# RWKV-6 attention and mixture of depths on one core: order of the state update, the gate's arithmetic, and where groups of product pieces end

## The chip, the cores and the metric

The kernel runs on one core of one Trainium2 chip, in FP32 but for a few BF16 comparison tables. The core has a matrix engine (TensorE; "PE" in the profile, with "PEld" for its weight loads), a vector engine (VectorE, "DVE"), a scalar engine (ScalarE, "ACT"), a general one (GpSimd, "POOL") and a queue for transfers (SyncE, "SP"). Each works through its own list of instructions in order, and they meet at semaphores. The metric is the device time of one execution in microseconds; each quoted time is a median over executions.

## The reference

Batch is 4, with 8 heads, 768 steps and 48 channels per head. The first part is a recurrence with a decaying state for each head, the second lets the 128 best of the 768 rows of each batch through a two-layer network.

```python
for t in range(S):                                   # attention
    cur = einsum('bhd,bhe->bhde', u[None] * kt, vt)
    y[:, :, t] = einsum('bhd,bhde->bhe', rt, state + cur)
    state = wt[:, :, :, None] * state + einsum('bhd,bhe->bhde', kt, vt)

x = y as rows of H*D = 384 values                    # bridge
scores = einsum('bsd,d->bs', x, w_gate)
for b in range(B):                                   # mixture of depths
    top_idx = argpartition(-scores[b], 128)[:128]
    xe = x[b, top_idx]                               # 128 x 384
    ye = maximum(xe @ w1, 0.0) @ w2                  # 384 -> 1024 -> 384
    g = 1.0 / (1.0 + exp(-scores[b, top_idx]))
    out[b, top_idx] = xe + g[:, None] * ye           # other rows: out = x
```

## The kernel before, in words

**Chunks and turns.** The 768 steps of a batch are cut into 6 chunks of 128 steps, so there are 24 chunks. The program is one long sequence of calls of `turn(i)`, i from -2 to 24, whose order is written by hand; every engine gets its instructions in that order. Turn i works on several chunks at different stages. In the order of the calls: `own_products(i+1)` (POOL), `scores(i)` (PE: products of R and K into the PSUM tile `ps_s`), `masked(i)` (DVE: two multiplications by a triangular mask, L292), `carry(i-1)` (DVE: `mid`, L379, the sum of the chunk's product tile `ps_kv` and the old state; then POOL multiplies by the decay, L380; for the first chunk of a batch DVE does it in one multiplication, L382; for the last there is nothing), `scaled(i+1, "K")` (PE transposes, DVE multiplies, L258), `back(i)` (PE transposes K back, ACT copies it out as `kt`, L297), `rows_out(i-1)` (PE `ps_y`, ACT, POOL, and the store), `row_products`, `compared_t(i-2)` (PE transposes the row scores into `ps_e`, L400), `own_values(i)` (ACT L270, POOL `vo` L274), `compared(i-2)` (DVE counts the larger scores), then one step of `mixture` and a first portion of network pieces, `scaled(i+1, "R")`, `decays_t(i+2)`, `outputs_t(i)` (PE L310 and L318, ACT `yt` L323), `carry_products(i)` (PE `ps_kv`), a second portion of pieces, `scans(i+2)` (DVE: two scans over the decays, L227 and L239, with two small operations between), `range_check(i+2)`, `row_sums(i-1)` (ACT L345) and a second step of `mixture`.

**PSUM.** The tiles `ps_kv` and `ps_e` share one bank (pool `psK`, one buffer), so `ps_e` of a turn can be written once `carry` has read `ps_kv`. The four kinds of transposes use two banks of `psT`. The network's `ps_h` and `ps_f` share one bank, `psM`, except in the last batch.

**The mixture.** `mixture(b)` is a generator, started when the last chunk of batch b is compared, and resumed twice per turn. Its steps are: rank, pick, the indices and the gathering of the 128 rows `xe` (an indirect transfer issued by POOL), an empty step, the transposes `xeT`, and the gate. The gate step computes the row score of `xe` again and the sigmoid of it, with exp of minus its absolute value: a multiply-and-sum over 384 columns (L482), four operations on one column each (L487, L492, L493, L495), one more (L498) on DVE and one exp on ACT (L490). Then the batch goes to the list `picked`. Counted from the turn in which the last chunk was compared, the gate falls into the third turn after it: turns 10, 16 and 22. For the last batch all this follows behind the turns.

**The pieces.** `forward(b)` is the network as a generator of 16 pieces. Eight are "h" pieces (three matrix products each); after every fourth, ACT empties the bank into `hid` with Relu (L516). Eight are "f" pieces (one product of 384 columns each, accumulated in the bank); after the last, DVE forms `ye` (L527) and POOL scatters it (L530). `fed(n)` takes n pieces from the batch in hand, or from the next one in `picked`. `fed_in_turn` calls it with 1 in the first portion of a turn and with 2 in the second (`PIECES` is 3); for the last batch but one it only takes one per turn.

**The end.** After turn 24 the last chunk is compared, four pieces run, the last batch is ranked, four more pieces run ahead of its indices, the rest of the third batch while its rows are fetched, and then the whole network of the last batch, alone.

Of the kernel before, what the change touches and what calls it, by code (L numbers as in the profile page):

```python
# [10 lines left out]
FP32 = mybir.dt.float32  # L11
# [3 lines left out]
AF = mybir.ActivationFunctionType  # L15
ALU = mybir.AluOpType
AX = mybir.AxisListType

L = 128
# [19 lines left out]
def kernel(  # L39
# [39 lines left out]
    nc = tc.nc  # L79
# [3 lines left out]
    C = H * D  # L83
# [14 lines left out]
    lev = ctx.enter_context(tc.tile_pool(name="lev", bufs=2))  # L98
    mod = ctx.enter_context(tc.tile_pool(name="mod", bufs=1))
# [43 lines left out]
    wg_bc = consts.tile([L, C], FP32)  # L143
# [276 lines left out]
    def mixture(b):  # L420

        every, ahead, lost = against.pop(b)
        ps = psT.tile([L, NCH], FP32, tag="t", name="ps_r")
        for c in range(NCH):
            for e in range(c, NCH):
                nc.tensor.matmul(
                    ps[:, c:c + 1], ahead[:, e, c * L:(c + 1) * L], ones[:, 0:1],
                    start=(e == c), stop=(e == NCH - 1),
                )
        rank = mod.tile([L, NCH], FP32, name="rank", bufs=2)  # L430
        nc.vector.tensor_add(rank, lost[:, :, 0], lost[:, :, 1])
        nc.vector.tensor_add(rank, rank, behind_n)
        nc.vector.tensor_sub(rank, rank, ps)
        yield

        for gi, (c0, n) in enumerate(groups):

            pick = mod.tile([L, NCH, L], BF16, name="pick")
            at = rank
            if c0 > 0:  # L440
                at = mod.tile([L, NCH], FP32, name="at")
                nc.vector.tensor_scalar_add(out=at, in0=rank, scalar1=float(-c0))
            nc.vector.tensor_tensor(
                out=pick, in0=_heads(slots, NCH), in1=at.to_broadcast([L, NCH, L]),
                op=ALU.is_equal,
            )
            yield
            ps = psT.tile([L, 2], FP32, tag="t", name="ps_i")
            for c in range(NCH):
                nc.tensor.matmul(  # L450
                    ps, pick[:, c, :], ids[:, b, c, :], start=(c == 0), stop=(c == NCH - 1)
                )
            while len(picked) + len(feed) > 1:
                fed(1)
            idx = mod.tile([L, 1], UINT32, name="idx", bufs=2)
            nc.vector.tensor_scalar(
                out=idx, in0=ps[:, 0:1], scalar1=ps[:, 1:2], scalar2=float(b * S),
                op0=ALU.add, op1=ALU.max,
            )
            rows = views[b][0:b + 1].rearrange("b s c -> (b s) c")  # L460
            where = bass.IndirectOffsetOnAxis(ap=idx[0:n, 0:1], axis=0)
            xe = mod.tile([L, C], FP32, name="xe", bufs=2)
            if n < L:
                nc.vector.memset(xe, 0.0)
            nc.gpsimd.indirect_dma_start(
                out=xe[0:n], out_offset=None, in_=rows, in_offset=where,
                bounds_check=(b + 1) * S - 1, oob_is_err=False,
            )
            yield
            yield  # L470

            ps = psT.tile([L, NDC, L], FP32, tag="t", name="ps_x")
            for dc in range(NDC):
                nc.tensor.transpose(ps[:, dc, :], xe[:, dc * L:(dc + 1) * L], ident)
            xeT = mod.tile([L, NDC, L], FP32, name="xeT", bufs=2)
            nc.scalar.copy(out=xeT, in_=ps)
            yield


            own = mod.tile([L, 1], FP32, name="own", bufs=2)  # L480
            scr = lev.tile([L, C], FP32, tag="scr", name="scr")
            nc.vector.tensor_tensor_reduce(  # L482
                out=scr, in0=xe, in1=wg_bc, scale=1.0, scalar=0.0, op0=ALU.mult, op1=ALU.add,
                accum_out=own,
            )
            neg = mod.tile([L, 1], FP32, name="neg", bufs=2)
            nc.vector.scalar_tensor_tensor(  # L487
                out=neg, in0=own, scalar=-1.0, in1=own, op0=ALU.mult, op1=ALU.min
            )
            nc.scalar.activation(out=neg, in_=neg, func=AF.Exp)  # L490
            den = mod.tile([L, 1], FP32, name="den", bufs=2)
            nc.vector.tensor_scalar_add(out=den, in0=neg, scalar1=1.0)  # L492
            nc.vector.reciprocal(out=den, in_=den)  # L493
            gate = mod.tile([L, 1], FP32, name="gate", bufs=2)
            nc.vector.scalar_tensor_tensor(  # L495
                out=gate, in0=own, scalar=0.0, in1=neg, op0=ALU.is_ge, op1=ALU.max
            )
            nc.vector.tensor_mul(gate, gate, den)  # L498
            picked.append((b, n, rows, where, xe, xeT, gate))
            yield  # L500

    def forward(b, n, rows, where, xe, xeT, gate):

        hid = mod.tile([L, NFC, L], FP32, name="hid")
        for f0 in range(0, NFC, 4):

            pool, tag = (psY, "y") if b == B - 1 and f0 % 8 == 4 else (psM, "m")
            ps = pool.tile([L, 4, L], FP32, tag=tag, name="ps_h")
            for q in range(4):
                for dc in range(NDC):  # L510
                    nc.tensor.matmul(  # L511
                        ps[:, q, :], w1[:, dc, (f0 + q) * L:(f0 + q + 1) * L],
                        xeT[:, dc, :], start=(dc == 0), stop=(dc == NDC - 1),
                    )
                if q == 3:
                    nc.scalar.activation(out=hid[:, f0:f0 + 4, :], in_=ps, func=AF.Relu)  # L516
                yield

        ps = psM.tile([L, C], FP32, tag="m", name="ps_f")
        for fc in range(NFC):  # L520
            nc.tensor.matmul(  # L521
                ps, hid[:, fc, :], w2[:, fc, :], start=(fc == 0), stop=(fc == NFC - 1)
            )
            if fc < NFC - 1:
                yield
        ye = mod.tile([L, C], FP32, name="ye", bufs=2)
        nc.vector.scalar_tensor_tensor(  # L527
            out=ye, in0=ps, scalar=gate, in1=xe, op0=ALU.mult, op1=ALU.add
        )
        nc.gpsimd.indirect_dma_start(  # L530
            out=rows, out_offset=where, in_=ye[0:n], in_offset=None,
            bounds_check=(b + 1) * S - 1, oob_is_err=False,
        )
        yield


    work = {}
    mixing, picked, feed = [], [], []

    def step(f, n, *more):  # L540
        if 0 <= n < N:
            f(work.setdefault(n, dict(n=n)), *more)
# [7 lines left out]
            except StopIteration:  # L550
                mixing.pop(0)

    def fed(n):

        while n > 0:
            if not feed:
                if not picked:
                    return
                feed.append((picked[0][0], forward(*picked.pop(0))))
            try:  # L560
                next(feed[0][1])
                n -= 1
            except StopIteration:
                feed.pop(0)

    def fed_in_turn(n):

        if (feed or picked) and (feed or picked)[0][0] == B - 2:
            n = min(n, 1) if n < PIECES - PIECES // 2 else 0
        fed(n)  # L570

    PIECES = -(-2 * NFC * len(groups) // NCH)


    def turn(i):
        step(own_products, i + 1)
        step(scores, i)
        step(masked, i)
        step(carry, i - 1, work.get(i))
        step(scaled, i + 1, "K", k_bufs, "right")  # L580
        step(back, i)
        step(rows_out, i - 1, i == N)
        if i == N:
            row_scores_soon(work[N - 1], work[N - 1]["x"])
        else:
            step(row_products, i - 1)
        step(compared_t, i - 2)
        step(own_values, i)
        step(compared, i - 2)
        mix()  # L590
        fed_in_turn(PIECES // 2)
        step(scaled, i + 1, "R", r_bufs, "left")
        step(decays_t, i + 2)
        step(outputs_t, i)
        step(carry_products, i)
        fed_in_turn(PIECES - PIECES // 2)
        step(scans, i + 2)
        step(range_check, i + 2)
        if i < N:
            step(row_sums, i - 1)  # L600
        if 0 <= i - 2 < N and chunks[i - 2][1] == NCH - 1:
            mixing.append(mixture(chunks[i - 2][0]))
        mix()
        if i > -2:
            loads(i + 5)
        if i > 1:
            load_weights(1 if NCH > 2 else 100)
# [17 lines left out]
    def general(gen):  # L625
        u_t = gen.tile([D, H], FP32, name="u_t")
        nc.sync.dma_start(out=u_t, in_=u.rearrange("h d -> d h"))
        for b in range(B):
# [34 lines left out]
            for _ in mixture(b):  # L663
                pass
# [8 lines left out]
        out=wide, in0=ps[0:1, 0:1], scalar1=0.0, scalar2=None, op0=ALU.is_gt  # L673
# [30 lines left out]
```

## Time and profile before

| what | value |
|---|---|
| time, median of 3 runs | 237.0 us (235.15 to 237.57) |
| span of the profiled execution | 235.7 us |
| PE busy, share of the span | 87% |
| DVE busy | 74% |
| ACT busy | 60% |
| POOL busy | 56% |
| chain that ended last, by engine | PE 55%, DVE 20%, ACT 9%, issue 8% |

The starts of the turns can be read from PE's first product of `scores` in each turn (the L283 rows of the timeline), in us from the span's start:

| turn | 2 | 5 | 7 | 9 | 10 | 11 | 12 | 13 | 14 | 15 | 16 | 17 | 18 | 22 | 23 |
|---|---|---|---|---|---|---|---|---|---|---|---|---|---|---|---|
| starts at | 25.46 | 45.45 | 57.18 | 72.08 | 80.19 | 89.01 | 98.32 | 106.46 | 115.74 | 124.65 | 132.41 | 141.24 | 150.56 | 184.65 | 192.29 |

So a turn takes 6 to 9.3 us. Turns 10 to 15 and 16 to 21 are the two batches in which attention and network pieces are mixed throughout (52.22 and 52.24 us), and from 199 us on only the end is left: it takes 36 us and is mostly one dependent chain.

In a row of the timeline the first number is the start in us, the second the time in us from the first to the last of the instructions merged in it, and the bracket is the engine's idle time just before, with what ended it. In a row of the waits the three numbers are the idle time in total, the number of waits, and the longest.

### The profile page before, as it was taken

What the parts mean: (1) busy time and instruction counts of PE and PEld (TensorE: products, weight loads), DVE (VectorE), ACT (ScalarE), POOL (GpSimd) and SP (SyncE); (2) the same over time, 40 slices, a digit from 0 to 9 for tenths busy, and PEclk for the clock granted to TensorE, in tenths of its full rate; (3) what the DMA queues carried; (4) which work ended last, traced back from release to release, by engine and by line L of the source; (5) the groups of instructions that cost most, each with busy time, mean ns of one, the idle gap of its engine ahead of it and who ended that gap; (6) DMA issues with size and microseconds to landing.
All of it is one profiled execution on the core that took longest, in us unless ns stands there. A gap on an engine that the chain in (4) does not pass through costs nothing.

```text
span 235.7 us, 6339 instructions
## 1 busy us (share of the span) xinstructions
PE 205.4 (87%) x2290; PEld 170.0 (72%) x2290; DVE 173.3 (74%) x386; ACT 141.0 (60%) x666; POOL 132.4 (56%) x153
## 2 busy tenths in 40 slices
PE   2889999999898997989999997989999987688960
PEld 2678888888687796877877886877777876665830
DVE  6977888999999799697697899788698873423010
ACT  6357788889787766677476657685576656111200
POOL 2364778877856983674467883584368845003010
PEclk9999999999999999999999999999999999799995
DMA  8999999998999785848946965956621101001001
GB/s 123 182 166 174 196 189 247 207 230 170 231 218 215 201 176 75 152 88 118 151 97 107 176 128 66 171 114 93 100 70 33 70 33 36 33 0 61 9 0 49
DMA packets 105655, 29.20 MB, mean 124 GB/s; under 512 B 100496, under 2 KB 104848, under 8 KB 105616
## 3 DMA queue, kind: packets, MB, share of 16 engines
q1 hardware_dynamic: 105104, 27.14, 65.2%
q0 software_dynamic: 512, 1.57, 2.2%
q8 instruction: 20, 0.33, 0.6%
q14 instruction: 19, 0.16, 0.2%
HBM read 23.20 MB, written 5.51 MB: 122 GB/s over the span
## 4 chain that ended last, share of the span: by engine, by line
PE 55%; DVE 20%; ACT 9%; issue 8%; DMA 3%; POOL 2%; POOLq 0%
PE ps_t L214 11%; PE ps_s L283 8%; PE ps_yt L310 7%; PE ps_f L521 7%; PE ps_yt L318 6%; PE ps_h L511 6%; PE ps_w L214 4%; DVE sc L292 4%; DVE left L239 3%; ACT kt L297 3%; PE ps_kv L364 3%; DVE right_buf L227 3%; DVE R L258 2%; PE ps_e L400 2%; ACT junk L249 2%
## 5 line engine op out<-in xcount | busy, mean ns | idle before, releaser
L270 ACT ACTIVATE rk<-rk 128x48 f32<-128x48 f32 x192 | 43.7, 236 | 0.0
L292 DVE TENSOR_TENSOR sc<-ps_s,before_f 128x512 f32<-128x512 f32 x48 | 30.8, 683 | 17.2 <-PE ps_s L283 17.2
L270 ACT ACTIVATION_READ_ACCUMULATOR rk<-rk 128x1 f32 x192 | 37.3, 194 | 0.0
L335 POOL TENSOR_TENSOR x<-x,vo 128x384 f32<-128x384 f32 x23 | 23.0, 1000 | 19.5 <-ACT x L334 19.5
L239 DVE TENSOR_TENSOR_SCAN left<-ps_w,from_left 128x511 f32<-128x511 f32 x24 | 30.7, 1281 | 0.9
L283 PE MATMUL ps_s<-R,K 48*128 48x128 f32 x384 | 29.0, 292 | 0.8 <-DVE R L258 0.7
L227 DVE TENSOR_TENSOR_SCAN right_buf<-ps_w,from_right 128x511 f32<-128x511 f32 x24 | 29.1, 1211 | 0.7 <-PE ps_w L214 0.6
L323 ACT COPY yt<-ps_yt 128x512 f32<-128x512 f32 x24 | 14.1, 586 | 24.1 <-PE ps_yt L318 21.4
L263 POOL TENSOR_TENSOR rk<-r_buf,k_buf 128x384 f32<-128x384 f32 x24 | 24.2, 1006 | 7.4 <-DMA r_buf<-in_r_dram 7.2
L511 PE MATMUL ps_h<-xeT,w 128*128 128x128 f32 x192 | 27.1, 292 | 1.3 <-ACT hid L516 0.7
L283 PEld LDWEIGHTS ps_s<-R,K 48*128 48x128 f32 x384 | 24.3, 194 | 4.0 <-issue 1.6
L310 PE MATMUL ps_yt<-sc,v_buf 128*64 128x128 f32 x384 | 27.1, 285 | 0.0
L340 POOL TENSOR_TENSOR scr<-x,wg_bc 128x384 f32<-128x384 f32 x23 | 25.5, 1108 | 1.8
L511 PEld LDWEIGHTS ps_h<-xeT,w 128*128 128x128 f32 x192 | 24.7, 204 | 2.3 <-ACT hid L516 0.9
L297 ACT COPY kt<-ps_t 128x512 f32<-128x512 f32 x24 | 14.0, 583 | 20.1 <-PE ps_t L214 20.0
L521 PE MATMUL ps_f<-w,hid 128*128 128x384 f32 x64 | 23.9, 499 | 2.1 <-ACT hid L516 2.1
L264 POOL TENSOR_TENSOR rk<-rk,u_bc 128x384 f32<-128x384 f32 x24 | 24.1, 1002 | 2.5 <-DMA u_bc<-in_u_dram 0.7
L310 PEld LDWEIGHTS ps_yt<-sc,v_buf 128*64 128x64 f32 x384 | 21.2, 140 | 4.1 <-issue 3.7
L380 POOL TENSOR_TENSOR state<-mid,all 128x192 f32<-128x192 f32 x16 | 8.1, 506 | 27.8 <-DVE mid L379 27.8
L318 PE MATMUL ps_yt<-R,state 64*48 64x128 f32 x320 | 21.5, 274 | 0.3 <-POOL state L380 0.3
L274 POOL TENSOR_TENSOR vo<-v_buf,own 128x384 f32<-128x384 f32 x24 | 19.9, 828 | 1.9 <-ACT rk L270 1.9
L214 PE MATMUL ps_w<-ident,w_buf 128*128 128x128 f32 x96 | 15.8, 291 | 4.8 <-DMA w_buf<-in_w_dram 4.2
(98 smaller groups left out, 390.2 us busy)
## 6 DMA issues: line engine op xcount, KB each, us to landing
w_buf<-in_w_dram SPq DMA_DIRECT2D x24, 192.0 KB, 4.6
k_buf<-in_k_dram SPq DMA_DIRECT2D x24, 192.0 KB, 4.7
r_buf<-in_r_dram SPq DMA_DIRECT2D x24, 192.0 KB, 4.9
v_buf<-in_v_dram SPq DMA_DIRECT2D x24, 192.0 KB, 4.2
out_dram<-x SPq DMA_DIRECT2D x24, 192.0 KB, 2.3
w<-in_moe_w_dram SPq DMA_DIRECT2D x3, 512.0 KB, 5.8
w<-in_moe_w_dram SPq DMA_DIRECT2D x4, 384.0 KB, 4.9
u_bc<-in_u_dram SPq DMA_DIRECT2D x1, 192.0 KB, 4.6
```

The costliest lines, as they stand in the source:

```text
L214: nc.tensor.transpose(ps[:, j, :], src(j), ident)
L227: nc.vector.tensor_tensor_scan(out=flat[:, W - 2::-1], data0=wt[:, W - 1:0:-1], data1=from_right.rearrange("p j t -> p (j t)")[:, W - 2::- ...
L239: nc.vector.tensor_tensor_scan(out=left.rearrange("p j t -> p (j t)")[:, 1:W], data0=wt[:, 0:W - 1], data1=start.rearrange("p j t -> p (j ...
L263: nc.gpsimd.tensor_mul(rk, r_bufs[n % NBUF][:, :, 0:D], k_bufs[n % NBUF][:, :, 0:D])
L270: nc.scalar.activation(out=rk[:, h, :], in_=rk[:, h, :], func=AF.Copy, accum_out=o[:, h:h + 1])
L283: nc.tensor.matmul(ps[:, par, j, :], t["K"][rows, j, :], t["R"][rows, j, :], start=True, stop=True,)
L292: nc.vector.tensor_mul(t["sc"][:, par], ps[:, par], _heads(before_f, HP))
L310: nc.tensor.matmul(ps[DP * par:DP * par + DP, j, :], vt[:, 2 * j + par, :], t["sc"][:, par, j, :], start=(j == 0), stop=(old is None), ski ...
L318: nc.tensor.matmul(ps[DP * par:DP * par + D, j, :], old[rows, j, :], t["R"][rows, j, :], start=False, stop=True, skip_group_check=True,)
L340: nc.gpsimd.tensor_mul(t["scr"], t.pop("x"), wg_bc)
L511: nc.tensor.matmul(ps[:, q, :], w1[:, dc, (f0 + q) * L:(f0 + q + 1) * L], xeT[:, dc, :], start=(dc == 0), stop=(dc == NDC - 1),)
L521: nc.tensor.matmul(ps, hid[:, fc, :], w2[:, fc, :], start=(fc == 0), stop=(fc == NFC - 1))
```

## The change

It has three parts, all of them in the order or the engine of work; what is computed stays the same.

1. `carry(i-1)` is called ahead of `scores(i)` and `masked(i)` instead of behind them, so on DVE `mid` stands in front of the two masks. It is meant to free the bank for `ps_e` and to start the state's update sooner.
2. The gate's score is formed by a product on POOL and a sum by ACT's accumulator, the exp is taken of the negated score directly, and two operations on one column are left on DVE (an addition with a cap at 3e38, and the reciprocal). A `yield` between the exp and these two puts them at the turn's end, behind the scans, and `picked` gets the batch half a turn later than before.
3. In the turns, a portion of pieces ends early at a piece whose bank is then emptied: the fourth h piece of a group, and the last f piece. It is meant to keep PE from waiting in front of the next piece for that emptying.

```diff
@@ mixture
+            scr = lev.tile([L, C], FP32, tag="scr", name="scr")
+            nc.gpsimd.tensor_mul(scr, xe, wg_bc)
             own = mod.tile([L, 1], FP32, name="own", bufs=2)
-            scr = lev.tile([L, C], FP32, tag="scr", name="scr")
-            nc.vector.tensor_tensor_reduce(
-                out=scr, in0=xe, in1=wg_bc, scale=1.0, scalar=0.0, op0=ALU.mult, op1=ALU.add,
-                accum_out=own,
-            )
-            neg = mod.tile([L, 1], FP32, name="neg", bufs=2)
-            nc.vector.scalar_tensor_tensor(
-                out=neg, in0=own, scalar=-1.0, in1=own, op0=ALU.mult, op1=ALU.min
-            )
-            nc.scalar.activation(out=neg, in_=neg, func=AF.Exp)
-            den = mod.tile([L, 1], FP32, name="den", bufs=2)
-            nc.vector.tensor_scalar_add(out=den, in0=neg, scalar1=1.0)
-            nc.vector.reciprocal(out=den, in_=den)
+            nc.scalar.activation(out=scr, in_=scr, func=AF.Copy, accum_out=own)
+            nc.scalar.activation(out=own, in_=own, func=AF.Exp, scale=-1.0)
+            yield
             gate = mod.tile([L, 1], FP32, name="gate", bufs=2)
-            nc.vector.scalar_tensor_tensor(
-                out=gate, in0=own, scalar=0.0, in1=neg, op0=ALU.is_ge, op1=ALU.max
-            )
-            nc.vector.tensor_mul(gate, gate, den)
+            nc.vector.tensor_scalar(
+                out=gate, in0=own, scalar1=1.0, scalar2=3e38, op0=ALU.add, op1=ALU.min
+            )
+            nc.vector.reciprocal(out=gate, in_=gate)
             picked.append((b, n, rows, where, xe, xeT, gate))
@@ forward
-                yield
+                yield q == 3
...
             if fc < NFC - 1:
-                yield
+                yield False
...
-        yield
+        yield True
@@ fed
-    def fed(n):
+    def fed(n, on=True):
...
-                next(feed[0][1])
+                last = next(feed[0][1])
                 n -= 1
+                if last and not on:
+                    return
@@ fed_in_turn
-        fed(n)
+        fed(n, on=False)
@@ turn
         step(own_products, i + 1)
+        step(carry, i - 1, work.get(i))
         step(scores, i)
         step(masked, i)
-        step(carry, i - 1, work.get(i))
         step(scaled, i + 1, "K", k_bufs, "right")
```

The instruction lists show what follows from part 2 for the pieces. A batch's pieces start one turn later: turns 10 and 16 lose the three h pieces that they had of the newly picked batch. Turn 13 now holds two h pieces (the second ends its portion) where it held three f pieces, turn 15 holds three f pieces instead of one, and turn 16 the last two f pieces of the batch before, with `ye` on DVE between the product R and the scans (before, `ye` stood in turn 15, ahead of R). Turns 17 to 22 repeat this. In turn 22 the last two f pieces replace one h piece, and the rest of the third batch is one piece later at the end, so that six f pieces instead of five stand between the last batch's indices and its transposes.

More of the change, by code (lines that the diff above doesn't have):

```diff
@@ L477, in mixture @@
             yield
+            scr = lev.tile([L, C], FP32, tag="scr", name="scr")
+            nc.gpsimd.tensor_mul(scr, xe, wg_bc)
             own = mod.tile([L, 1], FP32, name="own", bufs=2)
-            scr = lev.tile([L, C], FP32, tag="scr", name="scr")
-            nc.vector.tensor_tensor_reduce(
-                out=scr, in0=xe, in1=wg_bc, scale=1.0, scalar=0.0, op0=ALU.mult, op1=ALU.add,
-                accum_out=own,
-            )
-            neg = mod.tile([L, 1], FP32, name="neg", bufs=2)
-            nc.vector.scalar_tensor_tensor(
-                out=neg, in0=own, scalar=-1.0, in1=own, op0=ALU.mult, op1=ALU.min
-            )
-            nc.scalar.activation(out=neg, in_=neg, func=AF.Exp)
-            den = mod.tile([L, 1], FP32, name="den", bufs=2)
-            nc.vector.tensor_scalar_add(out=den, in0=neg, scalar1=1.0)
-            nc.vector.reciprocal(out=den, in_=den)
-            gate = mod.tile([L, 1], FP32, name="gate", bufs=2)
-            nc.vector.scalar_tensor_tensor(
-                out=gate, in0=own, scalar=0.0, in1=neg, op0=ALU.is_ge, op1=ALU.max
-            )
-            nc.vector.tensor_mul(gate, gate, den)
+            nc.scalar.activation(out=scr, in_=scr, func=AF.Copy, accum_out=own)
+            nc.scalar.activation(out=own, in_=own, func=AF.Exp, scale=-1.0)
+            yield
+            gate = mod.tile([L, 1], FP32, name="gate", bufs=2)
+            nc.vector.tensor_scalar(
+                out=gate, in0=own, scalar1=1.0, scalar2=3e38, op0=ALU.add, op1=ALU.min
+            )
+            nc.vector.reciprocal(out=gate, in_=gate)
             picked.append((b, n, rows, where, xe, xeT, gate))
```

## The prediction

> **What bounds the kernel now.** I read the page first, then PE's timeline for the length of each turn, then the waits, then all engines around turn 16, where a gate is computed.
>
> ```profile
> PE 205.4 (87%) x2290; PEld 170.0 (72%) x2290; DVE 173.3 (74%) x386; ACT 141.0 (60%) x666; POOL 132.4 (56%) x153
> ...
> PE   2889999999898997989999997989999987688960
> ```
>
> PE is busy nearly throughout until slice 33, so a turn can only shrink by the gaps that PE still has. The waits say which these are:
>
> ```profile
> DVE sc L292 <- PE ps_s L283: 17.2, 16, 1.9
> PE ps_e L400 <- DVE mid L379: 3.9, 4, 1.4
> PE ps_e L400 <- ACT kt L297: 3.1, 11, 0.3
> PE ps_f L521 <- ACT hid L516: 2.1, 3, 0.7
> PE ps_e L400 <- DVE state L382: 1.0, 1, 1.0
> ```
>
> `ps_e` needs nothing from `kt`; it needs the bank that `mid` reads, and `mid` ends within 0.05 us of `kt` in those 11 turns (28.23 against 28.27 us in turn 2). So the first row of `ps_e` and the second are one wait, for `mid`. DVE meanwhile waits 17.2 us in front of the masks: it has room there.
>
> The largest gaps come from the gate. Turn 16, DVE:
>
> ```profile
> 136.53 1.01 DVE L482 CUSTOM_DVE_ANT_0 scr<-xe,wg_bc 128x384 f32<-128x384 f32 x1
> ...
> 137.59 0.84 DVE L487 SCALAR_TENSOR_TENSOR neg<-own 128x1 f32<-128x1 f32 x1
> ...
> 139.25 0.93 DVE L498 TENSOR_TENSOR gate<-gate,den 128x1 f32<-128x1 f32 x1
> 140.10 0.68 DVE L258 TENSOR_TENSOR R<-ps_t,left 128x512 f32<-128x512 f32 x1
> ```
>
> From 136.53 to 140.10, 3.57 us, R and the two scans behind it stand still. The masks and `mid` of turn 17 are late for it, and PE has this gap in turn 17:
>
> ```profile
> 143.26 0.60 PE L214 MATMUL ps_y<-ident,yt 128*128 128x128 f32 x4
> 145.22 0.29 PE L400 MATMUL ps_e<-ident,score 128*128 128x128 f32 x1 [1.36 <-DVE mid L379]
> ```
>
> Why an operation on one column takes 0.9 us is seen on POOL:
>
> ```profile
> 138.37 0.82 POOL L274 TENSOR_TENSOR vo<-v_buf,own 128x384 f32<-128x384 f32 x1
> 139.16 1.00 POOL L263 TENSOR_TENSOR rk<-r_buf,k_buf 128x384 f32<-128x384 f32 x1
> ```
>
> L498 ends at 140.18, `rk` at 140.16. And ACT, whose next work after `yt` waits for the scans:
>
> ```profile
> 139.22 0.59 ACT L323 COPY yt<-ps_yt 128x512 f32<-128x512 f32 x1 [0.56 <-PE ps_yt L318]
> 142.35 0.19 ACT L238 COPY left<-from_left 128x1 f32<-128x1 f32 x1 [2.55 <-DVE from_left L235]
> ```
>
> **What the Trainium skill says.** "SBUF — State Buffer", section "Who interferes with whom": a DVE instruction with two SBUF inputs contends with a GpSimd instruction that reads SBUF, the later one is blocked to the other's end, and with at most one SBUF input it is free. The trace agrees: L498 (two inputs) takes 0.93 us beside `rk` and 0.16 us at the end, where POOL is idle; L492 and L493 (one input) take 0.15 and 0.16 us at every place. The two new DVE operations have one input each. "Trace Analysis", section "Per-engine timelines": the window of a DVE or ACT instruction leaves out its wait for semaphores, so a blocked instruction shows as idle time in front of it; the 2.55 us above are such a case. "ScalarE: Activation LUTs", section "Table sets: the hidden batching unit": cheap functions are in every set, so exp and copy share one; the trace agrees with one table load in all (1.28 us, at the start).
>
> **Part 1, `mid` in front of the masks.** It adds and removes nothing on DVE; `mid` (0.35 us, 0.26 us from start to start) moves into the idle time there. Gain on PE:
> - Turns 2 to 4: after `ps_e`, PE's next transposes need `kt`'s bank anyway. In turn 1, which has no `ps_e`, they start 0.05 us after `kt`; in turn 2 at 28.50, 0.23 us after it. Gain 0.17 us a turn, 0.5 us in all.
> - Turns 5 to 8 hang on DVE (the chain goes from masks to K, R, scans and masks again, from 46.66 to 66.40). A reordered queue that never idles gains nothing, but `mid` falls into the last idle time ahead of it: 0.3 us. The 1.03 us that PE saves in turn 7 (`state`, L382) are lost again in turn 9, where K's transposes wait for `idx` at the end of DVE's queue and the state on POOL stands behind the gathering. Up to turn 10: 0.8 us.
> - Turns 13 to 15 and 19 to 21: a piece follows `ps_e`, so the whole gap goes. From `ps_y` to `ps_e` it is 0.88 us in turn 14 (117.77 to 118.65) and 0.44 us in turn 12, where nothing waits. Gain 0.44 us each.
> - Turns 11, 17 and 23: see part 2.
>
> **Part 3, ends of portions.** In turn 12 PE waits from 104.77 (an h piece takes 0.77 us there) to 105.62 for `hid`: 0.85 us, and again in turn 18. Now an h piece stands in that place, and the bank's emptying is behind us: ACT finishes its own-values at 103.4, so `hid` ends at 104.0, where the next h piece starts. Gain 0.85 us each. The other such waits are in the end and stay.
>
> **Part 2, the gate.** Take turn 10 with its first score product as 0 (80.19 in the trace). DVE no longer does the gate and PE no longer the three h pieces (3 x 0.7 = 2.1 us, which return elsewhere). PE: `kt`'s transposes at 2.0 (they wait for `xeT`), `ps_e` 2.9, R's transposes 3.3, `yt` products 4.3 and 5.3, `ps_kv` 6.35, so turn 11 starts at 6.95 instead of 8.82. Then the new chain: POOL adds x at 3.7 (ACT's copy ends at 3.63), row product 4.8, `vo` 5.75, the new product 6.55 to 7.6 (1.0 us by the L340 row; 1.6 us at worst). ACT sums it (L345: 0.5 us) and takes exp (L490: 0.20 us): to 8.4. Behind these on ACT stand `yt`, `left`, the two range checks, the row sums and `kt` of turn 11: 2.5 us from `yt` to `kt` by turn 2 (24.98 to 27.5), so `kt` runs from 11.0 to 11.6, though PE wants it at 9.1. On DVE gate and reciprocal (0.2 us each with the wait between) hold `mid` until 9.1 and the masks until 9.35; `ps_e` 9.65, one h piece, then PE waits for `kt` until 11.65. Then 0.9 us of transposes, two times 1.02 of `yt` products, 1.5 of pieces: turn 12 starts at 16.15 instead of 18.13.
>
> Turn 16 has in addition two f pieces (0.65 and 0.7 us): turn 17 starts at 8.0. `ye` waits on DVE for the last of them, 8.05 to 8.7, and behind it the two scans, so `left` ends at 11.5, gate and reciprocal at 11.85, `mid` 12.2, masks 13.4. ACT's `left` waits for the reciprocal of the decays at 10.2, `kt` ends at 12.95. PE: `ps_e` 12.3, h piece, transposes 13.05, `yt` products 14.0; turn 18 starts at 17.6 instead of 18.15.
>
> The other turns: 12 takes 8.14 - 0.85 = 7.3; 13 has two pieces instead of three: 9.28 - 0.44 - 0.7 = 8.14; 14: 8.91 - 0.44 = 8.47; 15 has two pieces more: 7.76 - 0.44 + 1.39 = 8.71. Together 32.6.
> - Turns 10 to 15: 16.15 + 32.6 = 48.8, before 52.22: 3.4 us.
> - Turns 16 to 21: 17.6 + 32.6 = 50.2, before 52.24: 2.0 us.
> - Turns 22 to 24: by the same working `ps_y` of the last chunk comes at 13.4 from turn 22's start instead of 14.23: 0.8 us.
> - The end: six f pieces instead of five ahead of `ps_x`; the five end at 215.0, the rows arrive at 215.3, a piece takes 0.69: 0.4 us lost. The last gate lies beside the h pieces (5.6 us).
>
> Sum: 0.8 + 3.4 + 2.0 + 0.8 - 0.4 = 6.6 us; 237.0 - 6.6 = 230.4 us.
>
> **The rivals.**
> - The new waits take most of it: ACT's queue behind the sum and DVE's behind `ye` cost more than I worked out. For it: both stand in front of work that PE needs within 3 us, and POOL has been as late as 1.6 us for L340. If three gate turns lose 1.3 us more each, 234.3 us; that is where the batches gain little but the bank waits. 20%.
> - The new waits hide: if POOL runs the product sooner or PE reaches turn 11 later, `kt` is not late, which is worth up to (11.65 - 10.4) = 1.25 us in turn 11 and as much again in 17: 227.9 us. Against it: POOL's order is fixed, and `vo` waits for all eight own-values. 13%.
> - Nothing moves: PE is the bound and pieces are only pushed along. Against it: the gaps of 1.36, 0.85 and 0.44 us are idle time on PE. 237 us. 6%.
> - Slower: the pushed pieces meet the blocked scans, turns 16 and 17 grow beyond 18.15 by 2 us, and the end by one piece: 2 x 2 + 0.7 - 0.8 above the old time, 241 us. For it: `ye` stands ahead of both scans. 6%.
> - The forecast has the rest, 55%.
>
> **Range and chances.** From the hidden waits' 227.9 to the first rival's 234.3: 227.8 to 234.4 us leaves out the two last cases and the tails. Faster by over 1% means under 234.6 us: 55 + 13 + half of the 20, and a little of the spread, 0.79; within 1% 0.14; slower 0.07.
>
> **What would show it.** Right: no wait of `ps_e` for `mid` in turns 13 to 15; L487 and L490 at 0.15 us each; PE waits for `kt` of 1 to 2 us in turns 11 and 17; `ye` in turn 16 with idle time in front of it; turn 11 about 7 us after turn 10. Wrong: turn 18 later than 18.2 us after turn 16, or a `yt` so late that `ps_y` stops PE for over 1 us.

## The result, and the profile after

| | before | after |
|---|---|---|
| median of the first comparison (4 and 4 runs) | 236.07 us | 226.84 us |
| ratio, 95% interval | | 0.9624 [0.9536, 0.9712] |
| median of a later comparison (43 and 6 runs) | 235.39 us | 226.97 us |
| ratio, 95% interval | | 0.9599 [0.9548, 0.9649] |
| span of the profiled execution | 235.7 us | 225.0 us |

The ratios were estimated from the fast executions of each comparison and are not quotients of the medians, which take all of them (226.97 to 235.39 would be 0.964).

The kernel became 8.4 us faster by the medians of the larger comparison. The forecast was 230.4 us with a range down to 227.8, so the gain was larger than the forecast and the time fell below the range.

The page of the kernel after, busy times and PE's slices:

```profile
PE 201.2 (89%) x2290; PEld 167.7 (75%) x2290; DVE 165.2 (73%) x366; ACT 141.7 (63%) x674; POOL 135.6 (60%) x157
...
PE   2889999999999897999999996999999998688950
```

DVE lost 8 us of work and 20 instructions, POOL gained 3 us and ACT 0.7 us, and PE has fewer slices below 9 in the middle. The waits of the kernel after (engine and line, whom it waits for, us in total, times, longest):

```profile
DVE ye L522 <- PE ps_f L516: 17.2, 4, 7.5
...
ACT scr L483 <- POOL scr L481: 8.1, 4, 2.2
...
PE ps_e L400 <- ACT scr L345: 3.1, 2, 1.8
```

The rows of `ps_e` waiting for `mid`, `kt` and `state` are gone, as is PE's wait for `hid` inside the turns. In their place `ps_e` waits twice, 3.1 us in all, for the row sum of L345 on ACT. PE in turn 17 of the kernel after (start, duration; the bracket is the idle time ahead):

```profile
136.70 0.60 PE L214 MATMUL ps_y<-ident,yt 128*128 128x128 f32 x4
139.08 0.32 PE L400 MATMUL ps_e<-ident,score 128*128 128x128 f32 x1 [1.78 <-ACT scr L345]
```

These two rows answer to those of before with the wait of 1.36 us for `mid`. DVE and ACT show what led to it:

```profile
134.79 0.62 DVE L522 SCALAR_TENSOR_TENSOR ye<-ps_f,gate,xe 128x384 f32<-128x384 f32 x1 [3.22 <-PE ps_f L516]
135.32 1.21 DVE L227 TENSOR_TENSOR_SCAN right_buf<-ps_w,from_right 128x511 f32<-128x511 f32 x1
...
136.76 0.18 DVE L235 RECIPROCAL from_left<-all 128x4 f32<-128x4 f32 x1
...
138.18 0.13 DVE L487 TENSOR_SCALAR gate<-own 128x1 f32<-128x1 f32 x1
138.34 0.16 DVE L490 RECIPROCAL gate<-gate 128x1 f32<-128x1 f32 x1
```

```profile
134.14 0.52 ACT L483 ACTIVATE scr<-scr 128x384 f32<-128x384 f32 x1 [1.97 <-POOL scr L481]
...
136.98 0.19 ACT L238 COPY left<-from_left 128x1 f32<-128x1 f32 x1 [1.52 <-DVE from_left L235]
...
138.43 0.51 ACT L345 ACTIVATE scr<-scr 128x384 f32<-128x384 f32 x1
```

`ye` (L522) waits 3.22 us on DVE for PE's last f piece; e7 below tests whether the scans behind it could have run in that time. So L235 ends at 136.94, ACT's `left` starts at 136.98, and behind `left` and the two range checks stands the row sum (138.43), from which `ps_e` takes its operand. In turn 11 there is no `ye`, and the same wait (1.29 us) remains from ACT's sum of the gate alone, which waits 1.97 us for POOL.

Here is where the time went. The kernel before was run once more (`e4_before_again`), and its profile is used, since its matrix clock matches that of the kernel after; the sections are differences between the same rows of the two profiles:

| section | before (e4) | after | gained | forecast |
|---|---|---|---|---|
| up to turn 2 | 24.71 | 24.64 | 0.07 | 0 |
| turns 2 to 9 | 54.76 | 53.64 | 1.12 | 0.8 |
| turns 10 to 15 | 52.22 | 48.74 | 3.48 | 3.4 |
| turns 16 to 21 | 52.23 | 49.91 | 2.32 | 2.0 |
| turn 22 to the last `ps_y` | 14.22 | 12.91 | 1.31 | 0.8 |
| last `ps_y` to the end | 35.26 | 35.16 | 0.10 | -0.4 |
| span | 233.4 | 225.0 | 8.4 | 6.6 |

### The profile page after: what moved, and what is told of

Same layout as the page of the kernel before. It is cut to its first block, busy times and chain, and to the rows that moved or that the text cites. A ratio compares the mean times of both kernels' runs of the same rounds, so it can differ in the third digit from the quotient of the medians.

```text
span 225.0 us, 6333 instructions
## 1 busy us (share of the span) xinstructions
PE 201.2 (89%) x2290; PEld 167.7 (75%) x2290; DVE 165.2 (73%) x366; ACT 141.7 (63%) x674; POOL 135.6 (60%) x157
## 3 DMA queue, kind: packets, MB, share of 16 engines
q0 software_dynamic: 512, 1.57, 2.3%
## 4 chain that ended last, share of the span: by engine, by line
PE 67%; DVE 16%; ACT 6%; POOL 4%; issue 3%; DMA 1%; POOLq 0%; DVEq 0%
PE ps_t L214 12%; PE ps_f L516 10%; PE ps_h L506 10%; PE ps_s L283 9%; PE ps_yt L310 8%; PE ps_yt L318 7%; PE ps_w L214 4%; PE ps_kv L364 4%; DVE right_buf L227 3%; DVE left L239 3%; DVE sc L292 3%; PE ps_y L214 2%; DMA w_buf<-in_w_dram 1%; ACT kt L297 1%; ACT junk L249 1%
## 5 line engine op out<-in xcount | busy, mean ns | idle before, releaser
L270 ACT ACTIVATION_READ_ACCUMULATOR rk<-rk 128x1 f32 x192 | 38.5, 200 | 0.0
L506 PE MATMUL ps_h<-xeT,w 128*128 128x128 f32 x192 | 25.3, 280 | 1.3 <-ACT hid L511 0.7
L340 POOL TENSOR_TENSOR scr<-x,wg_bc 128x384 f32<-128x384 f32 x23 | 24.9, 1081 | 1.8
L506 PEld LDWEIGHTS ps_h<-xeT,w 128*128 128x128 f32 x192 | 23.0, 193 | 2.3 <-ACT hid L511 0.9
L318 PEld LDWEIGHTS ps_yt<-R,state 64*48 64x48 f32 x320 | 16.4, 119 | 4.1 <-issue 2.9
```

Of the source, the lines that this page charges most:

```text
L270: nc.scalar.activation(out=rk[:, h, :], in_=rk[:, h, :], func=AF.Copy, accum_out=o[:, h:h + 1])
L318: nc.tensor.matmul(ps[DP * par:DP * par + D, j, :], old[rows, j, :], t["R"][rows, j, :], start=False, stop=True, skip_group_check=True,)
L340: nc.gpsimd.tensor_mul(t["scr"], t.pop("x"), wg_bc)
L506: nc.tensor.matmul(ps[:, q, :], w1[:, dc, (f0 + q) * L:(f0 + q + 1) * L], xeT[:, dc, :], start=(dc == 0), stop=(dc == NDC - 1),)
```

## The experiments

All ratios are to the kernel before, run in the same comparison.

| run | what | median us | ratio [95%] |
|---|---|---|---|
| e1_state | part 1 alone | 230.31 | 0.9781 [0.9699, 0.9863] |
| e2_gate | part 2 alone | 233.36 | 0.9911 [0.9877, 0.9946] |
| e3_ends | part 3 alone | 242.62 | 1.0264 [1.0164, 1.0363] |
| e4_before_again | before, unchanged | 235.06 | 1.0006 [0.9965, 1.0047] |
| e5_no_ends | parts 1 and 2 | 228.66 | 0.9707 [0.9648, 0.9765] |
| e6_sum_later | after, gate's sum later on ACT | 226.56 | 0.9600 [0.9536, 0.9664] |
| e7_scans_first | after, scans ahead of `ye` | 225.14 | 0.9539 [0.9476, 0.9603] |
| e8_both | e6 and e7 | 223.51 | 0.9471 [0.9386, 0.9557] |
| e9_ends_scans | part 3 alone, scans ahead of `ye` | 234.24 | 0.9928 [0.9901, 0.9955] |
| e10_before_warm | before, idle products on PE | 235.51 | 0.9967 [0.9939, 0.9995] |
| e11_both_warm | e8, idle products on PE | 223.68 | 0.9458 [0.9403, 0.9513] |
| e12_after_again | after, unchanged | 226.97 | 0.9599 [0.9548, 0.9649] |

### The three parts, each alone

Part 1 alone:

```diff
         step(own_products, i + 1)
+        step(carry, i - 1, work.get(i))
         step(scores, i)
         step(masked, i)
-        step(carry, i - 1, work.get(i))
```

> Part 1 alone: the call of carry in front of scores and masked, the rest as before. Theory A (the gain is the sum of the PE gaps that the prediction listed): ps_e waits for mid nowhere; 1.1 us up to turn 10, 0.44 us in each of turns 13 to 15 and 19 to 21, about 1.1 us in turns 11 and 17 since mid is no longer behind the masks there, 0.5 in turn 23: 6.4 us in all, 229.7 us, ratio 0.973. Rival B (the gate on DVE is the main loss): mid only moves into idle time, turns 11 and 17 stay at 9.3 us because the gate still holds R and the scans; 3.5 us, 232.5 us, ratio 0.985. The end (last chunk's x to ps_r) keeps the pieces' grouping of the kernel before; theory C (its slow TensorE clock at 203 to 207 us belongs to that grouping) expects the same slow 3 us there, A expects it in some executions only.

Measured: 230.31 us, about 4.9 us below the 235.2 us of before in that comparison, between the two theories and nearer to A. Turns 13 to 15 and 19 to 21 shrank by 0.46 to 0.48 us each (forecast 0.44), turns 2 to 4 by 0.14 or 0.15 (0.17), turn 7 by 0.51, turns 11 and 17 by 0.74. From turn 2 to the last `ps_y` the profile of e1 takes 167.13 us for 173.43 in e4, 6.3 us less, near the 6.4 of theory A; the median shows less of it, but the profile of e1 reaches turn 2 only at 25.43 us, for 24.71 in e4. The waits of `ps_e` for `kt` are gone together with those for `mid`, so the two were one wait, as the prediction read them. In turns 11 and 17 `ps_e` now waits 0.6 us each for the row sum of L345. So `mid` in front of the masks is the largest single part.

Part 2 alone is the new gate with its `yield`, in the old order of `carry` and with the old ends of portions:

```diff
+            nc.gpsimd.tensor_mul(scr, xe, wg_bc)
...
-            nc.vector.tensor_tensor_reduce(
...
+            nc.scalar.activation(out=scr, in_=scr, func=AF.Copy, accum_out=own)
+            nc.scalar.activation(out=own, in_=own, func=AF.Exp, scale=-1.0)
+            yield
```

> Part 2 alone: the gate by POOL, ACT and two DVE operations with the added yield; carry stays behind the masks and portions end by number alone, so the wait for hid comes back in turns 13 and 19 and ye stands in front of R again. Theory A: turns 10 and 11 take 16.2 us together as after the change (ps_e of turn 11 waits for the row sum that stands behind the gate's sum on ACT), turns 13 to 15 keep the wait for mid; 2.3 us in all, 233.8 us, ratio 0.990. Rival B (the gate on DVE is the main loss): 5 us or more, 231 us, ratio 0.979.

Measured: 233.36 us, as theory A had it. Turn 10 falls from 8.82 to 6.97 us and turn 12 from 8.14 to 7.22, but turn 13 grows to 10.28 and turn 15 to 9.10, where the pieces went. From turn 2 to the last `ps_y` that is 1.65 us less than in e4.

Part 3 alone:

```diff
-                yield
+                yield q == 3
...
-        yield
+        yield True
...
+                if last and not on:
+                    return
...
-        fed(n)
+        fed(n, on=False)
```

> Part 3 alone: portions of pieces end where a bank is emptied, the rest as before. Theory A: the wait of 0.85 us for hid goes in turns 12 and 18, but the last f piece falls into the second portion of turns 15 and 21, so ye waits on DVE in front of both scans and turns 16 and 22 get 2 us longer each: 2.3 us slower, 238.4 us, ratio 1.010. Rival D (ye in front of the scans hides): 1.7 us faster, 234.4 us, ratio 0.993.

Measured: 242.62 us, slower by 2.6%. The direction was theory A's, the size three times its forecast. Turns 12 and 18 do gain 1.6 us each, but turn 16 takes 13.91 us for 8.83 and turn 22 takes 10.09 for 7.64. DVE and PE of e3 at the end of turn 15 and in turn 16:

```profile
130.69 0.62 DVE L527 SCALAR_TENSOR_TENSOR ye<-ps_f,gate,xe 128x384 f32<-128x384 f32 x1 [3.22 <-PE ps_f L521]
131.22 1.21 DVE L227 TENSOR_TENSOR_SCAN right_buf<-ps_w,from_right 128x511 f32<-128x511 f32 x1
```

```profile
135.34 1.11 PE L214 MATMUL ps_t<-ident,K 128*128 128x128 f32 x4 [2.68 <-ACT xeT L476]
```

`ye` waits 3.22 us in front of the scans here too; ACT's `left` waits for the scans, `xeT` stands behind `left`, and K's transposes wait 2.68 us for `xeT`'s bank. The four transposes then take 1.11 us instead of the usual 0.60: PE's clock is 0.50 from about 134 to 141 us, behind the gap. Of the 5.08 us that turn 16 lost, 2.68 are the wait and the other 2.4 go with that clock. In turn 22 the same wait, 2.69 us, has no halved clock behind it and costs 2.45 us. From the last `ps_y` to the end e3 takes 2.4 us more than e4, and there too its clock is halved, from about 205.7 to 212.5 us. These two stretches are what the forecast of 2.3 us lacked: with 4.8 us for them it comes to 7.1, and the profiles of e3 and e4 are 7.2 us apart. Why the clock was halved at the end of e3 was not tested; before has such a stretch as well (below).

That chain was only read from the trace, so `e9_ends_scans` takes it away: the same kernel with `scans` in front of the second portion, which moves `ye` behind the scans on DVE and leaves PE's order alone.

```diff
+        step(scans, i + 2)
         fed_in_turn(PIECES - PIECES // 2)
-        step(scans, i + 2)
```

> The kernel before with part 3 alone (a portion of pieces ends where a bank is emptied) and with scans called ahead of the second portion. Part 3 alone gave 242.6 us; turn 16 took 13.91 us for 8.83 before, turn 22 10.09 for 7.64. Theory A (ye stands in front of the two scans in turns 15 and 21, the scans hold ACT's left, and left holds xeT, for which K's transposes of turn 16 waited 2.68 us on PE; the halved clock behind that is its consequence): turns 16 and 22 come back to about 8.8 and 7.6 us, turns 12 and 18 stay at 6.55: about 233.3 us, ratio to before 0.992. Rival (part 3 harms where it moves the pieces, whatever ye does): turn 16 stays over 11 us, 239 us or more, ratio 1.016 or more.

Measured: 234.24 us, ratio 0.9928 [0.9901, 0.9955]. Turn 16 takes 8.78 us, turn 22 8.12, turns 12 and 18 stay at 6.55. So what part 3 alone lost in the turns was `ye` in front of the scans and what hung on it, the halved clock of turn 16 included: from turn 16 to the last `ps_y` e9 takes 6.3 us less than e3. Another 2.7 us of the 8.4 between the two lie behind that, where e3 has the halved clock and e9 none, and may be chance. Without the harm, the ends of portions and the moved scans together are a small gain; moved scans alone were not run in the kernel before.

`e5_no_ends` asks what part 3 does together with the other two; against the kernel after it only has `fed(n)` instead of `fed(n, on=False)`.

> The changed kernel without part 3 (parts 1 and 2 together: mid in front of the masks, the new gate; a portion of pieces no longer ends at an emptied bank). Alone, part 1 gave a ratio of 0.978, part 2 of 0.991, part 3 of 1.026: their product is 0.995, and all three together gave 0.962. Theory A (part 3 is harmful with the old placing of the pieces, and useful with that of part 2): the wait for hid is back in turns 13 and 19 (0.85 us, and one piece of 0.7 us more in each), the pieces are lost from turns 16 and 22 with their ye in front of the scans (-1.2 and -0.7 us): about +1.2 us on the changed kernel, 228.0 us, ratio to before about 0.969. Rival D (part 3 is worth nothing or harms here too): at or below the changed kernel's 226.8 us, 0.962 or less.

Measured: 228.66 us. Turns 13 and 19 take 9.80 us for 8.21 (the wait for `hid` and one more piece), turns 16, 17 and 22 are shorter by 0.85, 0.74 and 0.85. From turn 2 to turn 23 that is 0.78 us more than in the kernel after, and from turn 23 to the end 0.5 us more, together near the 1.2 us of theory A. The medians are 1.8 us apart; ahead of turn 2 the profile of e5 is 1.0 us later as well, which belongs to the clock (below). The interval of e5 overlaps with that of the first comparison of the kernel after, so the size of the gain rests on the two profiles; they speak against rival D. So part 3 loses about 7 us alone and gains 1 to 2 us on top of parts 1 and 2. Part 3 with only one of the others was not run. The parts are not additive: 0.978 x 0.991 x 1.026 = 0.995, and together they give 0.96.

### What still stands in front of `ps_e`

Two reorderings of the kernel after, alone and together. `e6_sum_later`:

```diff
             nc.gpsimd.tensor_mul(scr, xe, wg_bc)
+            yield
             own = mod.tile([L, 1], FP32, name="own", bufs=2)
```

> The changed kernel with one more empty step between POOL's product of xe and the gate's weights and ACT's sum and exp: these two stand behind the row sums (L345) on ACT's queue, at the end of the turn, and the two operations on DVE go into the next turn. PE's order is the same. Theory A (in turn 11 ps_e waits 1.29 us for the row sum of L345, which stands behind the gate's sum, and that sum waits 1.97 us for POOL): turn 11 falls from 9.28 to about 8.0 us; turn 17 stays near 9.7, since there ACT's left waits for the scans behind ye all the same: in all -1.2 us on the changed kernel, 225.6 us. Rival (in the place of the sum another wait of equal length holds ps_e, for instance for yt's PE products or DVE's mid): turn 11 stays over 9 us, 226.8 us.

`e7_scans_first` moves `scans` as e9 does, in the kernel after:

> The changed kernel with scans called ahead of the second portion of pieces, so that in turns 16 and 22 ye stands behind the two scans on DVE's queue and not in front of them. PE's order is the same. Theory A (ye, waiting 3.22 us for PE in turn 16, holds the scans, these hold ACT's left, and left holds the row sum that ps_e of turn 17 needs): turn 17 falls from 9.76 to about 8.1-9.3 us (the lower end if ACT's sum is not late either), turn 23 a little as well: -1 to -1.6 us, about 225.4 us. Rival (the gate's sum on ACT alone is what is late, as in turn 11 where there is no ye): turn 17 stays within 0.5 us of turn 11's 9.28: -0.5 us or less, 226.4 us.

> The changed kernel with both edits: the gate's sum and exp behind the row sums on ACT, and scans ahead of the second portion of pieces. Theory A (the two queues are the whole of what is lost in turns 11 and 17): turns 11 and 17 both come down to about 8.0 us, -1.25 and -1.75 us, with a little in turn 23: 223.4 us. Rival (PE or DVE has no room there, another wait follows): no better than the better one of the two edits alone, about 225.4 us.

| | after | e6 | e7 | e8 |
|---|---|---|---|---|
| turn 11, us | 9.28 | 7.91 | 9.29 | 7.90 |
| turn 17, us | 9.76 | 10.26 | 8.16 | 7.77 |
| all other turns from 2 to 22 | | within 0.02 | within 0.02 | within 0.02 |

The medians are 226.56, 225.14 and 223.51 us for forecasts of 225.6, 225.4 and 223.4. Each edit shortens the turn that its theory names. e6 alone makes turn 17 longer by 0.5 us, since there the gate's sum now stands between the row sum and `kt` and both are late for the scans' sake; with the scans ahead this is gone too. PE and DVE of e8 at the place of the waits shown above:

```profile
133.72 0.60 PE L214 MATMUL ps_y<-ident,yt 128*128 128x128 f32 x4
134.16 0.27 PE L400 MATMUL ps_e<-ident,score 128*128 128x128 f32 x1
```

```profile
130.16 1.28 DVE L239 TENSOR_TENSOR_SCAN left<-ps_w,from_left 128x511 f32<-128x511 f32 x1
131.81 0.62 DVE L523 SCALAR_TENSOR_TENSOR ye<-ps_f,gate,xe 128x384 f32<-128x384 f32 x1 [0.36 <-PE ps_f L517]
```

`ye` starts where PE lets it, with 0.36 us of idle time instead of 3.22, and `ps_e` follows `ps_y` without a gap. In turns 11 and 17 of e8 PE has no idle time left, so these two queues held all that it still waited for there, and e8 at 223.51 us is below both kernels of this study.

### The time of the kernel before, and the clock

The forecast began from 237.0 us. Of 43 times of the kernel before in the last comparison, 29 lie between 234.7 and 235.8 us and 14 between 237.1 and 238.0. The profiled execution of before (237.43 us, in the upper group) and that of `e4_before_again` (235.16, in the lower one) differ in two places. One is the clock granted to PE at the end (first the clock's row of the page of before, then windows of 2 us: PE's busy time, matmuls in brackets, clock):

```profile
PEclk9999999999999999999999999999999999799995
```

```profile
203.00:205.00 2.00, 1.54 (x7) 0.63 0.00 0
205.00:207.00 2.00, 2.00 (x12) 0.52 0.00 0
```

In windows of 0.2 us it is 0.50 from about 203.5 to 206.9 us, 3.4 us in all. The same group of products in before, and then in `e4_before_again`:

```profile
203.46 3.90 PE L511 MATMUL ps_h<-xeT,w 128*128 128x128 f32 x18 [0.69 <-ACT hid L516]
```

```profile
202.73 2.27 PE L511 MATMUL ps_h<-xeT,w 128*128 128x128 f32 x18 [0.69 <-ACT hid L516]
```

> The kernel before once more, for the TensorE clock at its end (windows from the last chunk's x to ps_r) and at its start, and for the spread of its time. Theory A: the clock's slow stretch is a matter of the moment, so another execution may show none at the end, and then takes 1.5 us less there. Theory C: the slow stretch of about 3 us at 203 to 207 us is there again. Ratio 1.000 in any case.

The same program ran once with the halved stretch and once without, at a cost of 1.63 us. The stretch alone does not part the groups: the mean clock of a run is 0.982 to 0.984 in all 14 of the upper group, but also in 8 of the 29 of the lower one, where 20 have 0.990 to 0.992 and one 0.977. It does not belong to the old grouping of the pieces: `e12_after_again` has it too (the kernel after at about 195 us, where the first profile had none), and its turns 2 to 22 are the same to 0.02 us.

> The changed kernel once more, unchanged, to place its runs beside those of the kernel before by the clock at start and end. Theory W: turns 2 to 22 are the same to 0.1 us as in the first profile (7.22 us in turn 12, 9.3 in 11, 9.8 in 17), and only turns 0 and 1 and the stretch around 195 us differ; runs between 224.5 and 229 us. Rival: the turns themselves differ between executions.

The other place is the start: PE's 16 products of turn 0's scores take 2.08 us in every profile and 1.16 us from turn 2 on, and by the durations the change to the full rate falls between about 13 us (e2: turn 2 starts at 22.84) and about 19.6 us (e5: at 25.64). Before reaches turn 2 at 25.46 us and e4 at 24.71; these 0.75 us and the 1.63 at the end make up the 2.3 us between the two profiles. The Trainium skill, "TensorE: Matmul & The Clock Gate", section "Part 1: The HAM clock gate", says that an idle PE gets half its clock, that a free-running window of 3.413 us decides when it changes, and that the change therefore falls at another place in each execution. The halved clock of 0.50, its length of 3.4 us and the varying start agree with it. Two sizes do not, and here the measurement decides: the page lets the change vary by 0.5 us, where these profiles, with the same work on PE up to there, are over 6 us apart, and it gives half the clock after an idle window, where PE had been busy for 1.39 of the 3.4 us.

To test it, idle products were added to the kernel before, on a tile of ones, in the gaps at the start and behind the last turn:

```diff
+    def busy(pool, tag, n):
+        ps = pool.tile([L, HP, L], FP32, tag=tag, name="ps_d")
+        for _ in range(n):
+            nc.tensor.matmul(ps[:, 0, :], ones, ones, start=True, stop=True)
+
     with tc.manual_schedule():
+        busy(psM, "m", 26)
         for i in range(-2, N + 1):
             turn(i)
 
+        busy(psW, "w", 20)
```

> The kernel before with idle work for PE added and nothing else: 26 BF16 products of a tile of ones with itself at the very start (into the network's bank, never read), while PE waits for the first decays, and 20 more in the gap behind the last turn, where PE waits 1.39 us for the last comparison. Theory W (the time of the kernel before lies in two groups 2 us apart since the phase of the clock's windows decides when TensorE comes to its full rate, at 14 to 19 us, and whether it falls to half of it for 3.4 us at 203 us): full rate before turn 0's scores in each execution, turn 2 starts at or ahead of 22.8 us for 24.7 and 25.5 before, no halved clock at the end: 232.5 us, all runs within 1 us, ratio 0.988. Rival C (the spread is from transfers or something else): two groups as before, or slower by what the added products take: 235 to 237 us.

> The changed kernel with the two reordered queues of the earlier run (the gate's sum behind the row sums on ACT, scans ahead of the second portion of pieces; 223.5 us, turn 2 at 23.02 us in its profile and halved clock at the end) and PE's idle work at the start and behind the last turn. Theory W: turn 2 at about 22.5 us, no halved clock at the end (-1.6 us): 221.5 us, ratio to before 0.942. Rival C: 223.5 us or above, 0.951 or more.

Half of theory W came true. The 22 times of e10 lie between 233.52 and 236.22 us: the group above 237 us, a third of the runs of before, is gone, and the profile shows no halved clock at the end. But the median, 235.51 us, did not fall, and the ratio, 0.9967 [0.9939, 0.9995], is only just below 1. The start of e10, rows and then windows:

```profile
1.07 2.95 PE L612 MATMUL ps_d<-ones 128*128 128x128 bf16 x26 [1.07 <-DVE ones L166]
...
9.42 2.08 PE L283 MATMUL ps_s<-R,K 48*128 48x128 f32 x16 [0.17 <-DVE R L258]
...
18.71 1.16 PE L283 MATMUL ps_s<-R,K 48*128 48x128 f32 x16
```

```profile
4.90:8.30 3.40, 1.57 (x11) 1.00 1.29 192
8.40:11.80 3.40, 3.23 (x22) 0.50 1.45 167
11.80:15.20 3.40, 2.72 (x13) 0.50 1.51 163
15.20:18.60 3.40, 3.40 (x36) 0.50 1.32 199
```

The added products did bring the full rate early: the transposes at 5.35 and 6.55 us take 0.63 us for the 1.09 and 1.08 of before. Then PE is busy for only 1.57 us of 3.4, the clock is halved at 8.4 us, and stays so until 18.7, about three windows. In the median the early gain was given back. Two of the 22 executions, at 233.52 and 233.66 us, have a mean clock of 0.993, where 16 have 0.970 to 0.972 like the profiled one (0.970): in those two the rate does not seem to have been lost again, and they are nearly 2 us below the median of before. That is read from the mean clocks; the profile is of one of the 16. e11 shows the same, 223.68 us for the 223.51 of e8: no gain that can be told. Rival C had the times right in both runs, though not its reason for e10, whose two groups did not stay. Nothing here keeps the start's gap between 4.9 and 8.3 us filled; that was not tried.

## Why the prediction was wrong, and where it was right

The forecast of 230.4 us was 3.6 us above the 226.84 measured. About half came from the time that it started from, the other half from small terms of its sum; either half put right alone would have brought the forecast to 228.8 or 228.6 us.

**The base, 237.0 us.** This step failed. The three times given, 237.0, 237.57 and 235.15, contained two from the smaller group, and the profile that the working was read from had the late start and the halved stretch at the end. With the median of 43 runs, 235.39 us, the same sum of 6.6 gives 228.8 us. No term of the sum, and no chance, stood for the clock; the page of before had one digit for it, a 7 in the clock's row for the slice from 200 us, and I read past it.

**The small terms.** The rest, 8.4 - 6.6 = 1.8 us, is spread over four terms that were all too low, in the table above:
- "The end: ... 0.4 us lost." Not lost: measured +0.10. From `ps_i` to `ps_x` it took 4.11 us with six pieces (200.72 to 204.83) and 3.98 with five (211.37 to 215.35). Six pieces took 4.12 us, 0.69 each as forecast, but the transposes' first record starts 0.17 us ahead of the last piece's end, and five pieces had left PE idle for 0.36 us: 0.13 us lost, and won back elsewhere.
- "Turns 22 to 24: ... 0.8 us." Measured 1.31. Part 1 alone gives 0.91 of it (in e1 it is 5.68 us from turn 23's start to the last `ps_y`, for 6.59). The rest is in turn 22, 7.22 us for 7.63, although it holds one piece more: turn 23's scores had waited 0.72 us for R, which stood behind the old gate, a wait that the prediction does not list. In e2, with the new gate alone, turn 22 falls by 0.85 us.
- "Turns 5 to 8 hang on DVE ... 0.3 us", and the 1.03 us of turn 7 lost again in turn 9: turn 7 became 0.54 us shorter and turn 5 0.14, and turn 9 gave nothing back (8.11 and 8.12).
- Turns 16 to 21: 2.32 for 2.0, of which turns 16 and 17 have 0.18 (17.42 for 17.6).

**Right.** Turns 10 to 15 were forecast at 48.8 us and took 48.74; single turns 12 to 15 at 7.3, 8.14, 8.47 and 8.71, and took 7.22, 8.21, 8.43 and 8.63. Part 1's 0.44 us a turn was 0.47 in e1. The wait of 0.85 us for `hid` in turns 12 and 18 is gone, L487 and L490 take 0.13 to 0.16 us, `ye` of turn 16 has idle time in front of it, and turn 11 starts 6.97 us after turn 10.

**Right in size, wrong in the name.** The forecast had PE wait 1 to 2 us for `kt` ahead of R's transposes in turns 11 and 17. It waits 1.29 and 1.78 us, but one step earlier, at `ps_e`, for the row sum of L345. The prediction gave `ps_e` only the bank as its need and left out its operand, the row score that L345 sums. Row sum and `kt` stand behind the same instructions on ACT, 0.5 us apart, and one h piece of 0.67 us stands between `ps_e` and R's transposes, so these start 11.72 us after turn 10's start, for 11.65 in the forecast. That it came so close is luck in part. e6, e7 and e8 confirm the two causes: the gate's sum in turn 11, `ye` ahead of the scans in turn 17.

**The rivals.** The new waits that take most of it, and the slower case with `ye` ahead of the scans, did not happen in the whole change, but e3 shows that the mechanism was real: with part 3 alone it costs 5.1 us in turn 16 and 2.5 in turn 22. The changed kernel escapes most of it because part 2 moves the last f pieces ahead of a turn in which no `xeT` stands behind `left`: K's transposes wait for nothing, in turn 16 and in turn 17. That reading of why it escapes is from the order and the trace alone.

## What to carry to other kernels

An instruction that waits for another engine should stand behind the work on its own queue that is ready, above all if a third engine hangs on that work: `ye` in front of two scans cost 6.3 us of turn time in one version, part of it by a halved clock, and 1.6 us in another, and one moved line repaired both. Judge the parts of a change together and apart, since a part that loses 7 us alone can gain with its neighbours. Before a forecast of a few per cent, look at how the given times are grouped: here the base was off by 1.6 us and all the small terms together by 1.8.

## What was not expected of the hardware

PE's clock was halved in some executions for 3.4 us near 203 us although no gap ahead of it was longer than 1.39 us: PE was busy 1.39 us of the 3.4 us from 200.0 to 203.4. With 1.28 us of idle products in that gap (2.43 busy of 3.4) the profile of e10 shows no halving; that of e4, without them, shows none either, so a single profile does not tell what prevents it. At the start of e10 the clock stayed at 0.50 for 10.2 us, through a stretch of 3.4 us in which PE was busy 3.23 us; why that was not enough stays open. The profile gives a granted clock of 1.00 for the first turns of before, where products take nearly twice as long as later (2.08 and 1.16 us): there the durations, not the clock's row, tell the rate.
